# Gate logits and phi(K) column sums: from 128-column to 512-column matmuls in a gated mix of softmax and linear attention

## The chip, the cores and the metric

The kernel runs on one core of a Trainium2 chip. The core has five engines that each work through a queue of their own: TensorE (PE, matmuls, with its weight loads shown as PEld), VectorE (DVE), ScalarE (ACT), GpSimd (POOL) and SyncE (SP, which issues transfers). They work on SBUF, and matmuls write into eight PSUM banks of 128 partitions x 512 fp32 values. The metric is the device time of one launch in microseconds (us); lower is better. Six runs of the kernel before gave a median of 783.94 us, from 782.10 to 785.14.

## The reference

The input x has 2048 rows of 512 values. Two attention blocks read it, both with 32 heads of 16 values, and a gate mixes their results row by row:

```
g = sigmoid((x * gate_w).sum(-1))               # one number per row
a = softmax(q k^T / 4) v, heads joined, @ A_wo   # q, k, v = x @ A_wqkv
phi(t) = where(t > 0, t + 1, exp(t)) + 1e-6
kv = phi(k)^T v        (16 x 16 per head)        # q, k, v = x @ B_wqkv
z  = sum over rows of phi(k)
b = (phi(q) kv) / (phi(q) z + 1e-6), heads joined, @ B_wo
out = g * a + (1 - g) * b
```

The change touches two small things of this: the 2048 gate logits `x . gate_w`, and the 512 sums `z` of phi(K) over the rows.

## The kernel before

**Softmax attention.** There are 32 rounds: 4 chunks of 512 queries, in each 4 groups of 8 heads, in each group the even and the odd heads (4 heads at a time). In a round, 16 blocks of 128 keys x 4 heads give 64 score tiles of 128 x 512, one PSUM bank each. PE makes a score tile with a 32-row matmul; four of them can run at once in different rows of the array. Banks 0 to 4 belong to ACT: it takes tiles in groups of three and two and turns them into exponentials (line 908). PE multiplies those by V into bank 7, where a round accumulates.

**VectorE's share of the exponentials.** VectorE claims whole key blocks of a round, from block 15 downwards. It moves four score tiles out of the spare banks 5 and 6, one or two banks at a time (line 1151), and forms the exponential by integer steps (lines 1174, 1177, 1180, 1183: the "chain"). Each block it claims takes four tiles off ACT; PE then needs three products with V in place of one.

**Everything else** is a list of tasks that use banks 5 and 6 as well: projections K, Q and V (`t_kproj`, `t_qproj`, `t_v0`, `t_v1`), the gate (`t_gate`), phi(K) (`t_phik`), its sums (`t_z`), the 512 x 512 product G = x^T phi(K) (`t_g`), and the tail of the linear block and the output. At the end of a round VectorE transposes bank 7 (`round_end`, line 998), and every second round a task divides by the softmax sum and multiplies by the gate (`t_norm`), which waits for the gate task and reads the gate in the layout of 32x32 blocks (`gT`, 128 x 64). The linear block's denominator (`t_den`) reads the other gate factor with a row per partition (`g1`, 128 x 16).

**The order** is written out by a planner when the program is built. It keeps a clock for each engine, adds the `cost` of every instruction, and at each step gives PE the best candidate that is ready. Each engine then runs its list in order, waiting on semaphores. A task has a due time and a time before which it may not start, in rounds (the two numbers of `add(...)`); tasks are tried in the order of their due times. When a task that is due within `RES` rounds still needs a bank (`pressed`, line 1081), VectorE's claims leave one of the two spare banks free. Where PE is found to have spare time, matmuls on a constant tile `warm` are inserted.

**The gate before.** `gwb` holds gate_w copied 128 times. For each of the 16 row blocks, 4 matmuls of 128 columns take x as the stationary operand and `gwb` as the moving one, so that each row's logit lands on its own partition, in 128 equal columns; the next row block is written one column further, and column tb remains. ACT forms exp(-logit) from PSUM (line 533), VectorE the sigmoid and its complement (lines 536 to 538), and sixteen copies of 32 partitions x 16 bring it into the block layout `gT` (line 542).

**The sums before.** `t_z` does the same: 64 matmuls of 128 columns with phi(K) as the stationary operand and a tile of ones as the moving one, and one copy of 128 x 4 (line 591). GpSimd then scales masks with it into `Zsel`, which `t_den` uses.

Of the kernel before, what the change touches and what calls it, by code (L numbers as in the profile page):

```python
# [7 lines left out]
ACT = mybir.ActivationFunctionType  # L8
ALU = mybir.AluOpType
FP32 = mybir.dt.float32  # L10
# [135 lines left out]
def bass_gated_mix__mha_block__linear_attn_block__prompt_kernel(  # L146
# [14 lines left out]
    NTB = S // 128  # L161
    NQC = S // 512
    NCC = D // 128
# [9 lines left out]
    with ExitStack() as es:  # L173
        def SB(name, shape, dt):
            return es.enter_context(nc.sbuf_tensor("sb_" + name, list(shape), dt))
# [4 lines left out]
        xT = SB("xT", [128, NCC, S], BF16)  # L180
# [30 lines left out]
        mtmp = SB("mtmp", [128, 8], FP32)  # L211
        mask8 = SB("mask8", [128, 8], FP32)
        blockmask = SB("blockmask", [128, 128], BF16)
        eg = SB("eg", [128, NTB], FP32)
        g0 = SB("g0", [128, NTB], FP32)
        g1 = SB("g1", [128, NTB], FP32)
        gT = SB("gT", [128, NTB * 4], FP32)
        rden = SB("rden", [128, 2, 16], FP32)
# [22 lines left out]
        R = _Res  # L241
# [39 lines left out]
        r_gw = R("gw")  # L281
        r_gwb = R("gwb")
        r_eg = R("eg")
        r_g0 = R("g0")
        r_g1 = R("g1")
        r_gT = R("gT")
        r_rden = R("rden")
# [6 lines left out]
        def op(E, fn, reads=(), writes=(), cost=0.2):  # L294
            if E is DV:
                ev = E.add(fn, _deps_for(E, reads, writes), cost=max(cost - 0.084, 0.05), lag=min(0.084, cost - 0.05))
            else:
                ev = E.add(fn, _deps_for(E, reads, writes), cost=cost, lag=0.12 if E is AC else 0.0)
            _record(E, ev, reads, writes)
            return ev  # L300
# [43 lines left out]
        def pe(fns, reads=(), writes=(), waves=1.0, m="full", cols=None):  # L344
            deps = _deps_for(PE, reads, writes) + fdeps
            fdeps.clear()
            n = len(fns)
            first = None
            cost = mcost(m, waves)
            mode[0] = m  # L350
            for k, fn in enumerate(fns):
                ev = PE.add(fn, deps if k == 0 else (), inc=(k == n - 1), cost=cost / n, lag=0.155)
                if k == 0:
                    first = ev
            first.t = ev.t
            c = 512.0 * waves if cols is None else cols
            hist.append((PE.clock, c))
            COLS.append((PE.clock, c))
            hsum[0] += c
            for res in reads:  # L360
                res.r[PE] = first
            for res in writes:
                res.w = ev
                res.r = {}
            if filler[0]:
                filler[0] = False
                lastf[1] = ev
            return ev

        def mm(o, l, r, start=True, stop=True, sg=False):  # L370
            return lambda: nc.tensor.matmul(o, lhsT=l, rhs=r, start=start, stop=stop, skip_group_check=sg)  # L371
# [75 lines left out]
        def proj_steps(b, lhs, rhs, reads, w=512):  # L447
            for h2 in range(2):
                yield ("pe", reads, [r_bk[b]] if h2 == 0 else [], 2 * w / 512)
                pe([mm(BK[b][:, 0:w], lhs(cc), rhs(cc), start=(cc == 0), stop=(cc == NCC - 1)) for cc in (2 * h2, 2 * h2 + 1)],  # L450
                   reads=reads, writes=[r_bk[b]], waves=2 * w / 512)
# [14 lines left out]
        def t_kproj(t8, t):  # L466
            if t8 == 0:
                lhs, wr = (lambda cc: wA0[:, 0, cc, :]), r_wA0[0]
            else:
                lhs, wr = (lambda cc: wA[:, 1, cc, 128 * t8:128 * (t8 + 1)]), r_wA[1]  # L470
            b = yield "bank"
            yield from proj_steps(b, lhs, lambda cc: xT[:, cc, 512 * t:512 * (t + 1)], [r_xT[c][t] for c in range(NCC)] + [wr])
            yield ("dve", [r_bk[b]], [])
            op(DV, lambda: nc.vector.tensor_copy(KT[:, t8, 512 * t:512 * (t + 1)], BK[b]), reads=[r_bk[b]],
               writes=[r_KT[t8][t]], cost=0.69)
            yield "free"
# [41 lines left out]
        def t_v1(tb):  # L518
            b = yield "bank"
            yield from proj_steps(b, lambda cc: xT[:, cc, 128 * tb:128 * (tb + 1)], lambda cc: wA[:, 2, cc, 128:512],  # L520
                                  [r_xT[c][tb // 4] for c in range(NCC)] + [r_wv1], w=384)
            yield ("dve", [r_bk[b]], [])
            op(DV, lambda: nc.vector.tensor_copy(V[:, tb, 8:32, 0:Dh], BK[b][:, 0:384].rearrange("p (h d) -> p h d", d=Dh)),
               reads=[r_bk[b]], writes=[r_V[tb][1]], cost=0.56)
            yield "free"

        def t_gate():
            b = yield "bank"
            for tb in range(NTB):
                yield ("pe", xt_all + [r_gwb], [r_bk[b]] if tb == 0 else [], 1.0)  # L530
                pe([mm(BK[b][:, tb:tb + 128], xT[:, cc, 128 * tb:128 * (tb + 1)], gwb[:, cc, :], start=(cc == 0), stop=(cc == NCC - 1))
                    for cc in range(NCC)], reads=xt_all + [r_gwb], writes=[r_bk[b]], waves=1.1, cols=512)
            op(AC, lambda: nc.scalar.activation(eg[:], BK[b][:, 0:NTB], ACT.Exp, scale=-1.0), reads=[r_bk[b]], writes=[r_eg], cost=0.2)
            yield "free"
            yield ("dve", [r_eg], [])
            op(DV, lambda: nc.vector.tensor_single_scalar(g1[:], eg[:], 1.0, ALU.add), reads=[r_eg], writes=[r_g1], cost=0.08)
            op(DV, lambda: nc.vector.reciprocal(g0[:], g1[:]), reads=[r_g1], writes=[r_g0], cost=0.2)
            op(DV, lambda: nc.vector.tensor_tensor(g1[:], eg[:], g0[:], ALU.mult), reads=[r_g0, r_eg], writes=[r_g1], cost=0.1)
            gv = gT[:].rearrange("p (t a) -> p t a", a=4)
            for j in range(4):  # L540
                for a in range(4):
                    op(DV, lambda j=j, a=a: nc.vector.tensor_copy(gv[32 * j:32 * j + 32, :, a], g0[32 * a:32 * a + 32, :]),  # L542
                       reads=[r_g0], writes=[r_gT], cost=0.08)

        epos = [0]

# [35 lines left out]

        def t_z():
            b = yield "bank"
            for i in range(4):
                for h in range(4):
                    yield ("pe", r_phiK + [r_const], [r_bk[b]] if i == 0 and h == 0 else [], 1.0)
                    pe([mm(BK[b][:, i:i + 128], phiK[:, tb, 128 * i:128 * (i + 1)], ones[:], start=(tb == 0), stop=(tb == NTB - 1))
                        for tb in range(4 * h, 4 * h + 4)], reads=r_phiK + [r_const], writes=[r_bk[b]], waves=1.1, cols=512)
            yield ("dve", [r_bk[b]], [])  # L590
            op(DV, lambda: nc.vector.tensor_copy(zsb[:], BK[b][:, 0:4]), reads=[r_bk[b]], writes=[r_z], cost=0.17)
            yield "free"
            for i in range(4):
                op(PO, lambda i=i: nc.gpsimd.tensor_scalar(Zsel[:, 8 * i:8 * i + 8], mask8[:], zsb[:, i:i + 1], None, op0=ALU.mult),
                   reads=[r_z, r_mask], writes=[r_Zsel], cost=0.2)
# [108 lines left out]
        def add(key, gen, due, nb=-1.0, pre=()):  # L704
            t = Task()
            t.pre = list(pre)
            t.key, t.gen, t.due, t.nb, t.seq = key, gen, due, nb, len(bykey)
            t.bank, t.done, t.started = None, False, False
            t.req = next(gen)
            tasks.append(t)  # L710
            bykey[key] = t
            tasks.sort(key=lambda k: (k.due, k.seq))
# [310 lines left out]
        lastd = [False]  # L1023
        FILL = 1
        FILLC = 5200
        RES = .2
        CHG = .2
        CHI = 0.1
        CHI2 = 0.1
# [184 lines left out]
            round_check()  # L1214


        V1D = .7
        V1N = .3
        V1S = .05
        K1D = .6  # L1220
        MH2 = .9
        GD = 1.9
        GN = 1.5
        XT = [("xtr", t) for t in range(NQC)]
        for t in range(NQC):
            add(("xtr", t), t_xtr(t), 0.25 * t - 0.3)
# [2 lines left out]
                add(("Q", 0, 0), t_qproj(0, 0), -0.19, pre=[("xtr", 0)])  # L1229
            add(("V0", t), t_v0(t), 0.25 * t - 0.15, pre=[("xtr", t)])  # L1230
        for tb in range(NTB):
            add(("V1", tb), t_v1(tb), V1D + 0.05 * (15 - tb), V1N + V1S * (15 - tb), pre=XT)
        add(("gate",), t_gate(), GD, GN, pre=XT)
        for t8 in range(1, 4):
            for t in range(4):
                if t8 == 1:
                    due = K1D + (0, 0.5, 0.7, 0.1)[t]
                    add(("K", t8, t), t_kproj(t8, t), due, due - 0.3, pre=XT)
                    continue
                add(("K", t8, t), t_kproj(t8, t), 2 * t8 - 0.9 + 0.1 * t, 2 * t8 - 1.8 + 0.2 * t,  # L1240
                    pre=XT)
        for q4 in range(1, 16):
            qc, t8 = divmod(q4, 4)
            due = K1D + 0.05 if q4 == 1 else 2 * q4 - 0.9
            add(("Q", qc, t8), t_qproj(qc, t8), due, due - 0.6, pre=XT)
        for tb in range(NTB):
            add(("phiK", tb), t_phik(tb), 100 + tb, 2.5 + 0.65 * tb, pre=XT)
# [162 lines left out]
```

The softmax here doesn't subtract the row's maximum and nothing guards it: scores larger than these inputs give would overflow.

## Time and profile before

| | before |
|---|---|
| median of 6 runs | 783.94 us (782.10 to 785.14) |
| the profiled execution's own time | 784.43 us |
| its span, first to last instruction | 782.5 us |
| mean granted TensorE clock | 0.988 |
| ACT busy | 758.5 us, 97% |
| PE busy | 744.1 us, 95% |
| VectorE busy | 703.7 us, 90% |
| ACT exponentials of scores (line 908) | 653, 749.8 us |
| blocks claimed by VectorE (line 1180) | 104 |
| gate matmuls | 64, from 79.1 to 85.0 us |
| matmuls for z | 64, from 329.3 to 336.2 us |
| gate copies (line 542) | 16, 173 ns each |

The profile shows one execution. A group line gives the line of the program, engine, operation, output and inputs, the count, then busy us and mean ns of one, then the idle time of that engine just before these instructions and what ended most of it. A timeline line gives the start, the length, the engine, the line and a count of merged instructions, with the idle time before it in brackets. A window line gives start and end, then for each engine the busy us and the number of instructions, then the clock that TensorE was granted (1.00 is full), the share of DMA time and GB/s. All matmuls are recorded under line 371, since one helper issues them; they are told apart by their operands.

### The profile page before, as it was taken

What the parts mean: (1) busy time and instruction counts of PE and PEld (TensorE: products, weight loads), DVE (VectorE), ACT (ScalarE), POOL (GpSimd) and SP (SyncE); (2) the same over time, 40 slices, a digit from 0 to 9 for tenths busy, and PEclk for the clock granted to TensorE, in tenths of its full rate; (3) what the DMA queues carried; (4) which work ended last, traced back from release to release, by engine and by line L of the source; (5) the groups of instructions that cost most, each with busy time, mean ns of one, the idle gap of its engine ahead of it and who ended that gap; (6) DMA issues with size and microseconds to landing.
All of it is one profiled execution on the core that took longest, in us unless ns stands there. A gap on an engine that the chain in (4) does not pass through costs nothing.

```text
span 782.5 us, 18236 instructions
## 1 busy us (share of the span) xinstructions
PE 744.1 (95%) x7950; PEld 224.8 (29%) x7950; DVE 703.7 (90%) x997; ACT 758.5 (97%) x690; POOL 9.7 (1%) x36
## 2 busy tenths in 40 slices
PE   8999899999999999999999999999999999999997
PEld 3332322222222222332223223222322322232222
DVE  4498889899999999989999999989999998898995
ACT  5999899999999999999999999999999999999996
POOL 4000000000000000000000000000000000000000
PEclk9999999999999999999999999999999999999999
DMA  7200000000000000102002000100010011001000
GB/s 186 73 7 1 1 8 2 8 2 8 2 6 3 2 8 1 36 2 60 3 2 61 2 8 10 28 28 2 20 29 15 9 22 34 8 13 23 2 2 28
DMA packets 31343, 14.95 MB, mean 19 GB/s; under 512 B 19104, under 2 KB 31264, under 8 KB 31264
## 3 DMA queue, kind: packets, MB, share of 16 engines
q1 hardware_dynamic: 29392, 13.00, 6.4%
q8 instruction: 63, 1.03, 0.5%
q10 hardware_dynamic: 1872, 0.79, 0.4%
q14 instruction: 16, 0.13, 0.1%
HBM read 6.55 MB, written 2.10 MB: 11 GB/s over the span
## 4 chain that ended last, share of the span: by engine, by line
ACT 75%; PE 17%; DVE 4%; issue 2%; DVEq 0%; POOL 0%; ACTq 0%; POOLq 0%
ACT sb_PT L908 73%; PE ps L371 17%; ACT sb_ebuf L550 2%; DVE sb_Lb L1151 1%; DVE sb_Xb L1180 1%; DVE sb_gT L542 0%; DVE sb_Xb L1174 0%; DVE sb_Lb L1183 0%; DVE sb_Eb L1177 0%; DVE sb_OT L1017 0%; DVE sb_Tn L1013 0%; DVE sb_xnat L554 0%; DVE sb_U L998 0%; ACT sb_wA L676 0%; DVEq L1360 0%
## 5 line engine op out<-in xcount | busy, mean ns | idle before, releaser
L908 ACT ACTIVATE sb_PT<-ps 128x1536 bf16<-128x1536 f32 (+1 forms) x653 | 749.8, 1402 | 13.9 <-PE ps L371 13.4
L371 PE MATMUL ps<-sb_QP,sb_KT 32*128 32x512 bf16 x2048 | 308.3, 387 | 28.5 <-ACT sb_PT L908 14.8
L1151 DVE TENSOR_SCALAR sb_Lb<-ps 128x512 uint16<-128x512 f32 (+1 forms) x287 | 265.2, 925 | 39.1 <-PE ps L371 37.6
L371 PE MATMUL ps<-sb_warm 128*17 128x512 bf16 (+8 forms) x2142 | 203.1, 343 | 1.3 <-POOL sb_warm L409 1.3
L371 PEld LDWEIGHTS ps<-sb_QP,sb_KT 32*128 32x128 bf16 x2048 | 77.1, 91 | 284.8 <-ACT sb_PT L908 214.9
L371 PE MATMUL ps<-sb_PT,sb_V 128*17 128x512 bf16 x1632 | 156.4, 388 | 1.8 <-DVE sb_U L998 1.6
L1180 DVE TENSOR_TENSOR sb_Xb<-sb_Xb,sb_Lb 128x2048 bf16<-128x2048 bf16 x104 | 126.6, 1218 | 0.0
L371 PEld LDWEIGHTS ps<-sb_warm 128*17 128x17 bf16 (+2 forms) x2142 | 61.6, 91 | 48.2 <-issue 25.4
L1174 DVE TENSOR_SCALAR sb_Xb<-sb_Lb 128x2048 uint16<-128x2048 uint16 x104 | 71.5, 688 | 1.2
L1183 DVE TENSOR_SCALAR sb_Lb<-sb_Lb 128x2048 uint16<-128x2048 uint16 x104 | 71.3, 686 | 0.0
L1177 DVE TENSOR_SCALAR sb_Eb<-sb_Lb 128x2048 uint16<-128x2048 uint16 x104 | 71.3, 686 | 0.0
L371 PEld LDWEIGHTS ps<-sb_PT,sb_V 128*17 128x17 bf16 x1632 | 37.4, 87 | 100.6 <-issue 91.4
L371 PE MATMUL ps<-sb_Lb,sb_V 128*17 128x512 bf16 x416 | 40.8, 383 | 0.2
L371 PE MATMUL ps<-sb_Eb,sb_V 128*17 128x512 bf16 x416 | 40.8, 383 | 0.2
L371 PE MATMUL ps<-sb_Xb,sb_V 128*17 128x512 bf16 x416 | 40.8, 383 | 0.1
L371 PE MATMUL ps<-sb_xT,sb_wA 128*128 128x512 bf16 x108 | 32.1, 392 | 0.1
L998 DVE STREAM_TRANSPOSE sb_U<-ps 128x512 f32<-128x512 f32 x32 | 22.7, 709 | 7.7 <-PE ps L371 7.7
L550 ACT ACTIVATE sb_ebuf<-ps 128x512 bf16<-128x512 f32 x32 | 24.9, 777 | 0.0
L371 PE MATMUL ps<-sb_xT,sb_wBx 128*128 128x512 bf16 x64 | 18.8, 384 | 0.6 <-DVE sb_xnat L554 0.4
L371 PE MATMUL ps<-sb_wA,sb_xT 128*128 128x128 bf16 (+1 forms) x128 | 19.0, 275 | 0.2
L371 PE MATMUL ps<-sb_phiK 128*128 128x512 bf16 x64 | 19.0, 383 | 0.0
L371 PE MATMUL ps<-sb_wBx,sb_xT 128*128 128x512 bf16 x64 | 18.5, 384 | 0.0
(80 smaller groups left out, 301.7 us busy)
## 6 DMA issues: line engine op xcount, KB each, us to landing
sb_QP<-sb_QT SPq DMA_DIRECT2D x120, 16.0 KB, 1.8
out_dram<-sb_wA SPq DMA_DIRECT2D x14, 128.0 KB, 1.7
sb_wA<-in_A_wqkv_dram SPq DMA_DIRECT2D x2, 512.0 KB, 6.3
sb_wBx<-in_B_wqkv_dram SPq DMA_DIRECT2D x2, 512.0 KB, 6.0
sb_xnat<-in_A_x_dram SPq DMA_DIRECT2D x2, 512.0 KB, 3.9
sb_phiK<-sb_wA SPq DMA_TRANSPOSE x64, 2.4
sb_xnat<-in_A_x_dram SPq DMA_DIRECT2D x3, 256.0 KB, 3.0
sb_wBv<-in_B_wqkv_dram SPq DMA_DIRECT2D x1, 512.0 KB, 8.9
```

What stands on the lines that cost most here:

```text
L371: return lambda: nc.tensor.matmul(o, lhsT=l, rhs=r, start=start, stop=stop, skip_group_check=sg)
L550: op(AC, lambda: nc.scalar.activation(ebuf[:, s, :], BK[b], ACT.Exp), reads=[r_bk[b]], writes=[r_e[s]], cost=0.48)
L908: op(AC, lambda: nc.scalar.activation(PT[:, slot, 0:512 * n], ps[:, 512 * set_[0]:512 * (set_[0] + n)], ACT.Exp, scale=SCALE), reads=wr, w ...
L998: op(DV, lambda: nc.vector.transpose(U[:, par, :], acc), reads=[r_acc], writes=[r_U[par]], cost=0.71)
L1151: op(DV, lambda: nc.vector.tensor_scalar(Lb[:, sl, 512 * k:512 * (k + n)], src, S1A, S1B, op0=ALU.mult, op1=ALU.add), reads=[r_bk[b] for b ...
L1174: op(DV, lambda: nc.vector.tensor_scalar(X, L, 0x7F, 0x3F00, op0=ALU.bitwise_and, op1=ALU.bitwise_or), reads=[rl], writes=[rx], cost=CH[0])
L1177: ev = op(DV, lambda: nc.vector.tensor_scalar(E_, L, 0xFF80, None, op0=ALU.bitwise_and), reads=[rl], writes=[re_], cost=CH[1])
L1180: ev = op(DV, lambda: nc.vector.tensor_tensor(xb, xb, lb, ALU.mult), reads=[rx, rl], writes=[rx], cost=CH[2])
L1183: ev = op(DV, lambda: nc.vector.tensor_scalar(L, L, float(EXP_SH), None, op0=ALU.add), reads=[rl], writes=[rl], cost=CH[3])
```

## The change

The gate now keeps `gwb` as the stationary operand and streams x: for each of the four 512-row chunks, 4 matmuls of 512 columns put the 512 logits into a bank, the same on all 128 partitions. VectorE transposes the bank in 32x32 blocks into `rowt`, and a copy of every 32nd column brings 16 columns of the chunk into `gl`; since all partitions were equal, this is already the block layout. The exponential on ACT, and sum, reciprocal and product on VectorE, run on 128 x 64 values; the reciprocal writes `gT` directly, and four copies of 32 partitions x 16 make `g1`. The sums z go the same way: `ones` is stationary, 16 matmuls of 512 columns stream phi(K), one transpose and four copies make `zsb`.

Four planner numbers change with it: `RES`, and the due times and earliest starts of the second V projection, the second K projection, the second Q projection and the gate.

```diff
         def t_gate():
-            b = yield "bank"
-            for tb in range(NTB):
-                yield ("pe", xt_all + [r_gwb], [r_bk[b]] if tb == 0 else [], 1.0)
-                pe([mm(BK[b][:, tb:tb + 128], xT[:, cc, 128 * tb:128 * (tb + 1)], gwb[:, cc, :], start=(cc == 0), stop=(cc == NCC - 1))
-                    for cc in range(NCC)], reads=xt_all + [r_gwb], writes=[r_bk[b]], waves=1.1, cols=512)
-            op(AC, lambda: nc.scalar.activation(eg[:], BK[b][:, 0:NTB], ACT.Exp, scale=-1.0), reads=[r_bk[b]], writes=[r_eg], cost=0.2)
-            yield "free"
+            for t in range(NQC):
+                b = yield "bank"
+                rd = [r_xT[c][t] for c in range(NCC)] + [r_gwb]
+                yield from proj_steps(b, lambda cc: gwb[:, cc, :], lambda cc: xT[:, cc, 512 * t:512 * (t + 1)], rd)
+                yield ("dve", [r_bk[b]], [])
+                op(DV, lambda b=b: nc.vector.transpose(rowt[:], BK[b]), reads=[r_bk[b], r_gl], writes=[r_rowt], cost=0.71)
+                op(DV, lambda t=t: nc.vector.tensor_copy(gl[:, 16 * t:16 * (t + 1)], rowt[:].rearrange("p (b c) -> p b c", c=32)[:, :, 0]),
+                   reads=[r_rowt], writes=[r_gl], cost=0.17)
+                yield "free"
+            op(AC, lambda: nc.scalar.activation(eg[:], gl[:], ACT.Exp, scale=-1.0), reads=[r_gl], writes=[r_eg], cost=0.2)
             yield ("dve", [r_eg], [])
-            op(DV, lambda: nc.vector.tensor_single_scalar(g1[:], eg[:], 1.0, ALU.add), reads=[r_eg], writes=[r_g1], cost=0.08)
-            op(DV, lambda: nc.vector.reciprocal(g0[:], g1[:]), reads=[r_g1], writes=[r_g0], cost=0.2)
-            op(DV, lambda: nc.vector.tensor_tensor(g1[:], eg[:], g0[:], ALU.mult), reads=[r_g0, r_eg], writes=[r_g1], cost=0.1)
-            gv = gT[:].rearrange("p (t a) -> p t a", a=4)
-            for j in range(4):
-                for a in range(4):
-                    op(DV, lambda j=j, a=a: nc.vector.tensor_copy(gv[32 * j:32 * j + 32, :, a], g0[32 * a:32 * a + 32, :]),
-                       reads=[r_g0], writes=[r_gT], cost=0.08)
+            op(DV, lambda: nc.vector.tensor_single_scalar(gl[:], eg[:], 1.0, ALU.add), reads=[r_eg], writes=[r_gl], cost=0.17)
+            op(DV, lambda: nc.vector.reciprocal(gT[:], gl[:]), reads=[r_gl], writes=[r_gT], cost=0.6)
+            op(DV, lambda: nc.vector.tensor_tensor(gl[:], eg[:], gT[:], ALU.mult), reads=[r_gT, r_eg], writes=[r_gl], cost=0.2)
+            gv = gl[:].rearrange("p (t a) -> p t a", a=4)
+            for a in range(4):
+                op(DV, lambda a=a: nc.vector.tensor_copy(g1[32 * a:32 * a + 32, :], gv[32 * a:32 * a + 32, :, a]),
+                   reads=[r_gl], writes=[r_g1], cost=0.16)
...
         def t_z():
             b = yield "bank"
-            for i in range(4):
-                for h in range(4):
-                    yield ("pe", r_phiK + [r_const], [r_bk[b]] if i == 0 and h == 0 else [], 1.0)
-                    pe([mm(BK[b][:, i:i + 128], phiK[:, tb, 128 * i:128 * (i + 1)], ones[:], start=(tb == 0), stop=(tb == NTB - 1))
-                        for tb in range(4 * h, 4 * h + 4)], reads=r_phiK + [r_const], writes=[r_bk[b]], waves=1.1, cols=512)
+            for h in range(8):
+                rd = r_phiK[2 * h:2 * h + 2] + [r_const]
+                yield ("pe", rd, [r_bk[b]] if h == 0 else [], 2)
+                pe([mm(BK[b], ones[:], phiK[:, tb, :], start=(tb == 0), stop=(tb == NTB - 1)) for tb in (2 * h, 2 * h + 1)],
+                   reads=rd, writes=[r_bk[b]], waves=2)
             yield ("dve", [r_bk[b]], [])
-            op(DV, lambda: nc.vector.tensor_copy(zsb[:], BK[b][:, 0:4]), reads=[r_bk[b]], writes=[r_z], cost=0.17)
+            op(DV, lambda b=b: nc.vector.transpose(rowt[:], BK[b]), reads=[r_bk[b], r_gl], writes=[r_rowt], cost=0.71)
+            rv = rowt[:].rearrange("p (i j c) -> p i j c", i=4, j=4)
+            for j in range(4):
+                op(DV, lambda j=j: nc.vector.tensor_copy(zsb[32 * j:32 * j + 32, :], rv[32 * j:32 * j + 32, :, j, 0]),
+                   reads=[r_rowt], writes=[r_z], cost=0.16)
             yield "free"
...
-        RES = .2
+        RES = .5
...
-        V1D = .7
+        V1D = 1.3
         V1N = .3
-        V1S = .05
-        K1D = .6
+        V1S = .06
+        K1D = 1.3
         MH2 = .9
         GD = 1.9
-        GN = 1.5
+        GN = .5
...
-            add(("V1", tb), t_v1(tb), V1D + 0.05 * (15 - tb), V1N + V1S * (15 - tb), pre=XT)
+            add(("V1", tb), t_v1(tb), V1D + (0.05 * (15 - tb) if tb > 12 else V1S * (tb + 4)), V1N, pre=XT)
...
-                    due = K1D + (0, 0.5, 0.7, 0.1)[t]
-                    add(("K", t8, t), t_kproj(t8, t), due, due - 0.3, pre=XT)
+                    due = K1D + (0.3, 0.55, 0.8, 0)[t]
+                    add(("K", t8, t), t_kproj(t8, t), due, V1N, pre=XT)
...
-            due = K1D + 0.05 if q4 == 1 else 2 * q4 - 0.9
+            due = K1D + 0.25 if q4 == 1 else 2 * q4 - 0.9
```

More of the change, by code (lines that the diff above doesn't have):

```diff
@@ L213, in bass_gated_mix__mha_block__linear_attn_block__prompt_kernel @@
         blockmask = SB("blockmask", [128, 128], BF16)
-        eg = SB("eg", [128, NTB], FP32)
-        g0 = SB("g0", [128, NTB], FP32)
+        rowt = SB("rowt", [128, 512], FP32)
+        eg = SB("eg", [128, NTB * 4], FP32)
+        gl = SB("gl", [128, NTB * 4], FP32)
         g1 = SB("g1", [128, NTB], FP32)
@@ L283, in bass_gated_mix__mha_block__linear_attn_block__prompt_kernel @@
         r_eg = R("eg")
-        r_g0 = R("g0")
+        r_rowt = R("rowt")
+        r_gl = R("gl")
         r_g1 = R("g1")
```

## The prediction

> **What bounds the kernel now.** I read the page first: the busy shares, then the costliest groups.
>
> ```profile
> PE 744.1 (95%) x7950; PEld 224.8 (29%) x7950; DVE 703.7 (90%) x997; ACT 758.5 (97%) x690; POOL 9.7 (1%) x36
> ...
> L908 ACT ACTIVATE sb_PT<-ps 128x1536 bf16<-128x1536 f32 (+1 forms) x653 | 749.8, 1402 | 13.9 <-PE ps L371 13.4
> ```
>
> ScalarE (ACT) is the bound: 749.8 us of softmax exponentials, and only 13.9 us of idle in front of them. So a time can change in two ways: that idle, or the number of exponentials. The second is the trade that VectorE offers: each of the 104 key blocks that it claims (104 instructions of line 1180) takes four of the 2048 score tiles off ACT. The groups' other columns (shapes kept apart) count 326 exponentials of three tiles and 327 of two, 1632 tiles; the chain of waits shows 25 in a row (62 or 63 tiles) in 28.05 us from 537.07, 0.449 us a tile, so **a block is worth 1.80 us of ACT**. On VectorE it fills about 5.33 us, by the starts of successive instructions (0.60 for each of seven, 1.13 for the multiply).
>
> Next I asked where the 13.4 us of waiting lie: ACT's waits are ten, and 5.83 of them is the start. Windows of 5 us show the largest of the rest, behind the gate:
>
> ```profile
> core 0: us, PE busy (x) PEld busy (x) DVE busy (x) ACT busy (x) POOL busy (x), PEclk, DMA share, GB/s
> 80.00:85.00 5.00, 4.96 (x71) 3.49 (x67) 5.00 (x9) 5.00 (x6) 0.00 (x0) 1.00 0.02 3
> 85.00:90.00 5.00, 4.91 (x58) 1.27 (x55) 3.47 (x17) 5.00 (x7) 0.00 (x0) 1.00 0.00 0
> 90.00:95.00 5.00, 1.87 (x16) 0.52 (x18) 4.71 (x13) 2.97 (x3) 0.00 (x0) 0.94 0.00 0
> 95.00:100.00 5.00, 5.00 (x26) 0.84 (x26) 3.64 (x6) 2.80 (x3) 0.00 (x0) 0.50 0.00 0
> 100.00:105.00 5.00, 5.00 (x49) 1.29 (x47) 3.96 (x7) 4.77 (x5) 0.00 (x0) 0.88 0.04 11
> ```
>
> ACT is full to 90 us and loses 4.46 us in the next 15. TensorE (PE) is busy 1.87 of 5 us, and then runs at half clock. The timeline says why:
>
> ```profile
> 87.69 3.23 DVE L542 COPY sb_gT<-sb_g 32x16 f32<-32x16 f32 x16
> ...
> 90.95 0.69 DVE L1151 TENSOR_SCALAR sb_Lb<-ps 128x512 uint16<-128x512 f32 x1
> ...
> 91.79 0.40 PE L371 MATMUL ps<-sb_QP,sb_KT 32*128 32x512 bf16 x4 [1.88 <-DVE sb_Lb L1151]
> ...
> 92.23 2.37 ACT L908 ACTIVATE sb_PT<-ps 128x1536 bf16<-128x1536 f32 x2 [1.63 <-PE ps L371]
> ...
> 94.38 0.60 PE L371 MATMUL ps<-sb_PT,sb_V 128*17 128x512 bf16 x4 [1.33 <-DVE sb_U L998]
> ...
> 95.58 2.52 ACT L908 ACTIVATE sb_PT<-ps 128x1536 bf16<-128x1536 f32 x2 [0.98 <-PE ps L371]
> ...
> 99.67 2.53 ACT L908 ACTIVATE sb_PT<-ps 128x1536 bf16<-128x1536 f32 x2 [1.57 <-PE ps L371]
> ```
>
> Sixteen gate copies hold VectorE's queue for 3.23 us (0.20 apart, written into the program as 0.08 each). Behind them waits the line 1151 that frees a score bank; PE stands 1.88 us for it, and 1.33 us for the late transpose; the slow clock follows. ACT's waits here are 1.63, 0.98, 1.57 and 0.17: **4.35 us, all one event**. Three later ones (0.81, 0.78, 0.86 at 449, 568 and 711 us) are not near anything that changes.
>
> Here a page and the trace differ. The Trainium skill (TensorE: Matmul & The Clock Gate, "Why this matters for your kernels") wants no PE-idle gaps over about 3 us; here none exceeded 1.88 us and the clock still fell to 0.50. By the page's rule only the 1.63 would belong to the copies and the gain would be that much; I go by the trace's 4.35.
>
> **The change, part by part.**
>
> *PE.* Gate: 64 matmuls of 128 columns become 16 of 512. In a run, 16 of the first take 1.05 us (79.72 to the next group at 80.76), so 64 take 4.2; four 512-column ones from 31.11 last 1.03, of which the last takes 0.39, so 0.21 apart and 3.4 in all. 0.8 us less, and again 0.8 for z (64 to 16). ACT covers it: 5.00 of 5.00 busy while the gate's matmuls run, and no ACT wait between 326 and 345 us. Taken as 0; ends -1.6 and 0. The same skill page ("Wait — 56ns, not 53.3ns?") gives 55.6 and 215.7 ns, an estimate of only 0.1 us a task; nothing above needs it.
>
> *VectorE, gate.* Removed: 87.11 to 90.92, 3.81 us for 19 instructions. Added: four transposes of a bank, the form of line 998 (0.709), each with a copy behind it that waits for it (0.17 to 0.20, like the small gate instructions); with 0.03 of hand-over, 0.94 a pair, 3.76. Then the add (0.20), the reciprocal of 64 elements (0.253 for 16 and 0.953 for 128 give 0.55), the product (0.174 for 16, 0.293 for 128: 0.23) and three hand-overs, 1.08; four 32-partition copies at 0.20, 0.81. Sum 5.65, 1.84 more.
> *VectorE, z.* One copy (0.154) becomes a transpose and four copies, 0.74 + 0.81 = 1.55: 1.40 more. POOL's Zsel starts that much later; it ends at 338 us and the first denominator is finished at 479, so 140 us cover it.
> Each of the five transposes waits in VectorE's queue for its matmuls, and line 1151 pieces stand behind it; the casts of K (line 474) wait likewise, 1.0 us for nine after 30 us, so 0.11 apiece, 0.55 for five, which is 0.2 us of ACT and inside the ends below. The gate held one of the two spare banks from 79.1 to 85.8; it now holds one four times for some 2 us, which I count as equal.
> Together 3.2 us. VectorE is 90% busy, in the middle rounds 95%, so I make it pay in blocks: 3.2/5.33 x 1.80 = **+1.1 us** (ends: 0 if it fits its 79 us of idle; 3.6 for two whole blocks).
>
> *The stall.* The added pieces are larger but come as 4 x 0.94, separated by the matmuls of the next quarter, and a tail of 1.9; the costs written for them (0.71, 0.17, 0.6, 0.16) are near the rows, so the written order of PE no longer runs 2 us ahead of VectorE. **-4.35 us** (ends: -4.86, with the 0.51 wait at 78.21; -2.7, if PE's first wait of 1.63 stays and only the slow clock goes). What is late next is the exponential below.
>
> *A new wait.* Line 533 read PSUM straight behind PE and waited for nothing. Now ACT's gate exponential waits in ACT's queue for VectorE's last copy, and all softmax exponentials stand behind it. VectorE may be in a multiply (1.22) ahead of transpose and copy (0.88): 2.1, less the one exponential that ACT has in hand (1.19 or 1.61): **+0.6 us** (ends 0 and 2.1), once.
>
> *The order written for rounds 1 to 3.* V1 keeps 16 casts of 0.554 us and their matmuls, but key blocks 0, 1, 2 ... come due first, as the second head group eats them (three for VectorE's claims ahead), not last; K1's dues move too. Between 33 and 130 us VectorE finishes 10 blocks; at the later 20 per 130 us it would be 15; its 13.8 us of idle from 30 to 130 (86.2 busy by windows of 10 us) hold two blocks at most. I take half a block, **-0.9 us** (ends -3.6 and +1.8, a block lost). Every Q task's eight DMAs stay; they move with their dues.
>
> *RES .2 to .5.* A bank is kept from VectorE earlier before each due task. I take 0: a task that gets the bank starts at once. Its price is a rival below.
>
> Sum: -4.35 + 1.1 + 0.6 - 0.9 + 0 = -3.55 us. The profiled execution took 784.43 (span 782.5 and 1.93 around it), so 780.9 against it; it stood 0.49 above the median, 783.94, and against that **780.4**.
>
> **Rivals.**
> *A: the sum*, 780.4. Chance 0.45, its own range 777.5 to 782.8.
> *B: the order gains more.* The two blocks come that VectorE's early idle has room for, and not half: 2.7 more, 777.7; with the new wait fully hidden 777. For it: 40 single-bank pieces of line 1151 against 3 pairs between 30 and 130 us, 8.1 us idle before them. Against: PE is 5.00 of 5.00 there. Chance 0.20.
> *C: the stall moves.* Another late VectorE piece stops PE at another place, as at 449, 568 and 711 us without any gate; a fresh order may carry four more of about 0.85, 3.4, and 783.8 is left. Chance 0.14.
> *D: slower, the kept bank.* One round is 782.5/32 = 24.4 us, so RES keeps a bank up to 0.3 x 24.4 = 7.3 us longer for each of 27 K and Q tasks, if the task leaves it unused. In that time VectorE starts 1.1 blocks, 2.2 pairs of tiles that become singles: 2 x (0.686 + 0.17 idle) - (1.218 + 0.09) = 0.40 us each, 24 us in all, 4.5 blocks, 8.1 us: 788.5 at worst. It outweighs the sum's gain from 44% of that; at 75%, 786.5. For it: 129 pairs are there to be split, and PE's order has PE and ACT ahead of such tasks. Against: a free bank costs a task nothing to take. Chance 0.21.
> That PE's saving shortens nothing is part of all four.
>
> **How the numbers follow.** A measurement of this kernel tells about 0.2% (1.6 us) from no change. Faster: nearly all of A and all of B, 0.65. Same: C's middle and A's weak edge, 0.13. Slower: D and C's bad edge, 0.22. Range: down to 774.5 (B with VectorE's extra work and the wait both hidden, 1.7 less, and PE's 1.6), up to 787.5, most of D; the gains and losses share it, A's own range stands above.
>
> **What the profile after would show.** The sixteen copies gone; the ACT wait behind the gate under 1 us and the clock 1.00 through 85 to 105 us; four line-998-like transposes of 0.71 for the gate and one for z; a short ACT idle before the gate's exponential, released by VectorE; line 1180 at 103 to 105. Wrong: a count of 101 or less with more single-bank 1151s (D), new PE waits with half clock elsewhere (C), or 106 and more (B).

## The result and the profile after

The changed kernel takes 779.59 us (median of 19 runs), the kernel before 783.48 us in the same sessions (42 runs). The ratio, taken over all runs, is 0.9955, 95% interval [0.9945, 0.9964]: about 0.45% faster; that of the two medians is 0.9950. The forecast was 780.4 against 783.94, a ratio of 0.9955 as well. How much of that agreement was earned is the question of the rest. Of all executions below only two lie far outside, 1188 and 816 us, both of the last kernel of section 6: its time leaves them out, and as the profiled one is among them, its waits aren't known.

The page of the changed kernel, engine totals and the exponentials (busy us, share of the span; idle before them and what ended it):

```profile
PE 741.6 (95%) x7817; PEld 220.1 (28%) x7817; DVE 706.8 (91%) x999; ACT 757.8 (97%) x690; POOL 10.2 (1%) x36
...
L916 ACT ACTIVATE sb_PT<-ps 128x1536 bf16<-128x1536 f32 (+1 forms) x653 | 749.4, 1414 | 9.3 <-PE ps L373 9.1
...
L1188 DVE TENSOR_TENSOR sb_Xb<-sb_Xb,sb_Lb 128x2048 bf16<-128x2048 bf16 x104 | 126.6, 1218 | 0.0
```

There are still 653 exponentials and 104 claimed blocks. The span is 4.6 us shorter (777.9 after 782.5), and most of it is idle time: 9.3 us in front of the exponentials, where it was 13.9. VectorE has 3.1 us more to do. PE has 2.5 us less, but not by the shorter gate: the matmuls of gate and z are busy 9.4 us before and 9.3 after, and the filler on `warm` went from 203.1 to 194.1.

Behind the gate, windows of 5 us of the changed kernel (start:end, then for each engine busy us and instructions, then TensorE's clock, DMA share, GB/s):

```profile
75.00:80.00 5.00, 4.85 (x46) 1.61 (x38) 4.59 (x13) 4.00 (x6) 0.00 (x0) 1.00 0.00 0
80.00:85.00 5.00, 4.61 (x41) 1.09 (x39) 4.95 (x9) 4.68 (x5) 0.00 (x0) 1.00 0.00 0
85.00:90.00 5.00, 5.00 (x54) 1.69 (x53) 3.76 (x7) 4.65 (x5) 0.00 (x0) 1.00 0.01 3
90.00:95.00 5.00, 4.88 (x43) 1.27 (x39) 3.65 (x7) 5.00 (x5) 0.00 (x0) 1.00 0.00 0
95.00:100.00 5.00, 5.00 (x45) 1.37 (x42) 5.00 (x9) 5.00 (x6) 0.00 (x0) 1.00 0.07 17
```

PE is never below 4.61 of 5 us and its clock stays at 1.00. ACT still loses 1.67 us here, in four pieces (0.66, 0.34, 0.32, 0.35); its timeline names them (start, length, line, idle before and what ended it):

```profile
76.88 0.26 ACT L539 ACTIVATE sb_eg<-sb_gl 128x64 f32<-128x64 f32 x1 [0.66 <-DVE sb_gl L536]
...
78.82 3.28 ACT L916 ACTIVATE sb_PT<-ps 128x1024 bf16<-128x1024 f32 x3 [0.34 <-PE ps L373]
82.42 6.89 ACT L916 ACTIVATE sb_PT<-ps 128x1536 bf16<-128x1536 f32 x6 [0.32 <-PE ps L373]
89.65 21.79 ACT L916 ACTIVATE sb_PT<-ps 128x1536 bf16<-128x1536 f32 x19 [0.35 <-PE ps L373]
```

The 0.66 is the new wait of the gate's exponential for VectorE. The other waits after the start are 0.18 at 42 us (and 0.22 at 23.5, as before), 0.39 and 0.63 near 237 us, 0.89 at 470 us.

### The profile page after: what moved, and what is told of

It reads as the page before. It is cut to its first block, busy times and chain, and to the rows that moved or that the text cites. A ratio compares the mean times of both kernels' runs of the same rounds, so it can differ in the third digit from the quotient of the medians.

```text
span 777.9 us, 17928 instructions
## 1 busy us (share of the span) xinstructions
PE 741.6 (95%) x7817; PEld 220.1 (28%) x7817; DVE 706.8 (91%) x999; ACT 757.8 (97%) x690; POOL 10.2 (1%) x36
## 4 chain that ended last, share of the span: by engine, by line
ACT 81%; PE 11%; DVE 5%; issue 2%; DMA 1%; SPq 0%; DVEq 0%; ACTq 0%
ACT sb_PT L916 79%; PE ps L373 11%; ACT sb_ebuf L554 2%; DVE sb_Lb L1159 2%; DVE sb_Xb L1188 1%; DMA sb_xT<-in_A_x_dram 1%; DVE sb_Eb L1185 0%; DVE sb_Xb L1182 0%; DVE sb_Tn L1021 0%; DVE sb_xnat L558 0%; DVE sb_U L1006 0%; DVE sb_OT L1025 0%; SPq L306 0%; DVE sb_Lb L1191 0%; ACT sb_wA L684 0%
## 5 line engine op out<-in xcount | busy, mean ns | idle before, releaser
L373 PE MATMUL ps<-sb_warm 128*17 128x512 bf16 (+8 forms) x2105 | 194.1, 341 | 1.3 <-POOL sb_warm L411 1.3
L373 PEld LDWEIGHTS ps<-sb_warm 128*17 128x17 bf16 (+2 forms) x2105 | 59.8, 91 | 49.6 <-issue 27.7
```

## The experiments

Two readings compete from the start. The theory: the order that is written out for PE believed the sixteen gate copies took 0.05 us each of VectorE, they take 0.20, and what follows in PE's list came up to 2.4 us too early; the change removes this mis-booking. Rivals: the new planner numbers made the gain (rival 1), or the shorter work did, the matmuls of 512 columns and the missing copies (rival 2). All times below are medians; every group of runs had its own runs of the kernel before beside it, from 783.26 to 783.48.

### 1. One number in the kernel before

```diff
-                       reads=[r_g0], writes=[r_gT], cost=0.08)
+                       reads=[r_g0], writes=[r_gT], cost=0.284)
```

(VectorE's booked time is the cost less 0.084 and at least 0.05.)

> The kernel before, with one number changed: the sixteen gate copies are booked at 0.20 us of VectorE's time each, as measured, where a written cost of 0.08 books 0.05. The work is the same. Theory (it is the lateness against the written order that stalls PE, not the 3.2 us of copies): ACT's waits behind the gate fall below 1.5 us, the clock stays at 1.00, about 780.5. Rival 2 (what counted is that the copies, or the 128-column matmuls, are gone): within 1 us of before, 783.5.

Measured: **779.46 us, ratio 0.9954 [0.9937, 0.9970]**: the whole gain of the change, with not one instruction changed in kind. Windows, and VectorE's timeline, of this kernel:

```profile
85.00:90.00 5.00, 4.95 (x59) 1.33 (x56) 3.47 (x17) 5.00 (x7) 0.00 (x0) 1.00 0.00 0
90.00:95.00 5.00, 4.07 (x34) 1.13 (x31) 4.48 (x12) 5.00 (x6) 0.00 (x0) 1.00 0.00 0
95.00:100.00 5.00, 5.00 (x42) 1.34 (x41) 4.11 (x7) 5.00 (x6) 0.00 (x0) 1.00 0.10 26
```

```profile
87.64 3.25 DVE L542 COPY sb_gT<-sb_g 32x16 f32<-32x16 f32 x16
90.92 0.35 DVE L1010 RECIPROCAL sb_rden<-sb_U 128x32 f32<-128x32 f32 x1
```

The copies still hold VectorE for 3.25 us, but no line 1151 stands behind them that PE waits for: the next instruction is the normalization. ACT is full, the clock stays at 1.00. The expected time was 780.5. Of the waits around the gate only the 0.51 at 78 us is left. But the gain is not the gate's alone: the three late waits (2.45 us in all) are gone too, and a new one came, 2.66 us of ACT at 333 us, where PE's list now runs fourteen matmuls of G in one go (the G burst):

```profile
332.31 3.19 PE L371 MATMUL ps<-sb_phiK,sb_xnat 128*128 128x512 bf16 x14
...
336.52 5.97 ACT L908 ACTIVATE sb_PT<-ps 128x1536 bf16<-128x1536 f32 x5 [2.66 <-PE ps L371]
```

### 2. The operations alone, and the numbers alone

The first kernel has the new `t_gate` and `t_z` with RES .2 and the old dues; the second the old two with RES .5 and the new dues.

> The new gate and z, with the planner numbers of before (RES .2, the old dues). Theory (the stall behind the sixteen gate copies was the loss): ACT's waits behind the gate fall from 4.35 us to under 1.5 us and the time to about 780, 0.4% below before. Rival 1 (the planner numbers made the gain): about 783.5, no change, with the waits moved and not gone.

> The gate and z of before, with the new planner numbers. Theory: the sixteen copies still hold VectorE 3.2 us, ACT still waits 3 us or more behind them, the time stays within 1 us of before, 782.5 to 784.5. Rival 1 (the planner numbers made the gain): about 779.6, with less than 1.5 us of ACT wait behind the gate.

The numbers alone: 783.18, ratio 1.0003 [0.9991, 1.0015], with 3.19 + 0.84 + 0.71 us of ACT waits behind the gate. As the theory had it. This execution also started late: its first wait is 7.50 us and not 5.83. The operations alone: **787.18, ratio 1.0053 [1.0035, 1.0071], slower**, which neither reading expected. The gate's waits shrank only to 0.51, 0.37 and 2.00 us. No sixteen copies are there, yet PE idles again behind the gate and its clock falls; its longest idle time in this stretch is 0.98 us, for a late transpose of bank 7:

```profile
90.00:95.00 5.00, 2.95 (x20) 0.79 (x18) 4.37 (x13) 5.00 (x7) 0.00 (x0) 0.99 0.00 0
95.00:100.00 5.00, 5.00 (x32) 0.78 (x28) 2.58 (x5) 3.17 (x3) 0.00 (x0) 0.50 0.07 16
```

```profile
94.87 0.60 PE L373 MATMUL ps<-sb_PT,sb_V 128*17 128x512 bf16 x4 [0.98 <-DVE sb_U L1006]
...
100.59 10.88 ACT L916 ACTIVATE sb_PT<-ps 128x1536 bf16<-128x1536 f32 x9 [2.00 <-PE ps L373]
```

The G burst was there again (2.04 us), and a new event at 569 us:

```profile
569.19 0.93 PE L373 MATMUL ps<-sb_phiK 128*128 128x512 bf16 x2 [3.17 <-DMA sb_phiK<-sb_wA]
...
570.71 2.52 ACT L916 ACTIVATE sb_PT<-ps 128x1536 bf16<-128x1536 f32 x2 [3.61 <-PE ps L373]
```

PE waits for DMA transposes of the linear block's output. On SyncE's queue they are issued from 562.54 us on, sixteen in 24.70 us, right behind eight QP transfers of 4.94 us; PE starts at 569.19, 6.65 us after the first was issued, so it does not wait for all of them. Neither half of the change gains by itself.

### 3. The copies brought back into the changed kernel

```diff
+            for j in range(4):
+                for a in range(4):
+                    op(DV, lambda j=j, a=a: nc.vector.tensor_copy(scr[32 * j:32 * j + 32, 16 * a:16 * a + 16], gT[32 * a:32 * a + 32, 0:16]),
+                       reads=[r_gT], writes=[r_scr], cost=0.08)
```

(`scr` is a scratch tile. In the second kernel the cost is 0.284.)

> The changed kernel with sixteen extra VectorE copies of 32 partitions x 16 into a scratch tile after the gate, booked at 0.05 us each as in before; nothing reads them. Theory: PE's written order runs some 2.4 us ahead of VectorE again, ACT waits 3 to 5 us behind the gate, about 783. If only VectorE's work counted, 3.2 us of it are 0.6 of a block: at most 1.1 us, 780.7. Rival 2 (the matmuls): 779.6.

> The same sixteen extra copies in the changed kernel as in the run with the copies brought back, but booked at 0.20 us of VectorE's time each, as they take. Theory (the written order ahead of VectorE is what costs): 779.5 to 781, with under 2.2 us of ACT wait behind the gate. Rival (3.2 us more work on VectorE cost the time): 783 or more, as when they were booked at 0.05.

Under-booked: 784.82, ratio 1.0022 [1.0006, 1.0038], 5.2 us above the changed kernel. The event is back where the copies are (79.59, 3.13 us on VectorE), with PE waiting 2.75 us, until 84.58, for a cast of V that stands behind them:

```profile
79.59 3.13 DVE L552 COPY sb_scr<-sb_gT 32x16 f32<-32x16 f32 x16
...
86.34 1.02 ACT L922 ACTIVATE sb_PT<-ps 128x1024 bf16<-128x1024 f32 x1 [2.70 <-PE ps L375]
...
88.71 2.36 ACT L922 ACTIVATE sb_PT<-ps 128x1536 bf16<-128x1536 f32 x2 [1.34 <-PE ps L375]
...
92.14 1.45 ACT L922 ACTIVATE sb_PT<-ps 128x1536 bf16<-128x1536 f32 x1 [1.07 <-PE ps L375]
```

Truly booked: the 2.70, 1.34 and 1.07 are gone, and the waits from 70 to 110 us add up to 2.04 (0.66, 0.35, 1.03). But the time is 783.26, ratio 1.0000 [0.9987, 1.0014]: the theory's number for the waits held and its number for the time did not. The new order brought the G burst (2.04) and a wait of 5.83 instead of 4.00 us at the tail. The 3.2 us of work cost no block: 104 again.

### 4. Which part of the numbers

The changed kernel with RES .2; then with RES .5 and the old dues:

> The changed kernel with RES back at .2. Theory (a bank kept early spares PE the forced finish of a half-done task, as in the G burst of 3.2 us seen around 333 us in two runs with RES .2): an ACT wait of 2 us or more returns with a burst of one task's matmuls, 781.5 to 784. Rival D of the prediction (a bank kept early costs VectorE pairs of tiles): more two-bank pieces than 127 and a time of 779 or less.

> The changed kernel with RES at .5, but the dues and earliest starts of the V, K and Q projections and of the gate as before. Theory (their order is worth half a block or less): 779.5 to 781, 104 blocks. Rival (their order is what lets the new gate pay): 784 or more, with ACT waits of 4 us or more between 75 and 105 us.

RES .2: **786.27**, ratio 1.0039 [1.0026, 1.0052]. The G burst costs ACT 2.05 us and the wait for the DMA transposes 3.97 + 1.34, as in the operations alone:

```profile
336.34 92.76 ACT L916 ACTIVATE sb_PT<-ps 128x1536 bf16<-128x1536 f32 x82 [2.05 <-PE ps L373]
568.17 2.53 ACT L916 ACTIVATE sb_PT<-ps 128x1536 bf16<-128x1536 f32 x2 [3.97 <-PE ps L373]
572.04 6.02 ACT L916 ACTIVATE sb_PT<-ps 128x1536 bf16<-128x1536 f32 x5 [1.34 <-PE ps L373]
```

Two-bank pieces (line 1151 taking two banks at once) are 129 against 127, and the blocks 104 in both: rival D's mechanism is there in sign (two pairs) and worth nothing. Old dues: 783.41, ratio 1.0003 [0.9989, 1.0016], between the two expectations. Around the gate it has the waits of the operations alone, 0.51, 0.38 and 2.00, with a clock of 0.50 from 95 to 100 us, and 103 blocks, one fewer. In the profiled executions ACT waits as long as in the changed kernel, 9.8 us in all; the block is 1.8 of the 2.7 us between the two spans, and the rest isn't explained.

### 5. True booking with the other numbers

The kernel before, with the true cost and RES .5; with the true cost and all the new numbers; with RES .5 alone:

```diff
-                       reads=[r_g0], writes=[r_gT], cost=0.08)
+                       reads=[r_g0], writes=[r_gT], cost=0.284)
...
-        RES = .2
+        RES = .5
```

> The kernel before with two numbers changed: the gate copies booked at 0.20 us and RES .5. Theory: the gate's waits stay gone, and the ACT wait of 2.66 us behind the G burst at 333 us goes too: 776.5 to 778, better than the changed kernel. If RES does nothing: 779.5. If the new matmuls were needed after all: 783.

> The gate and z of before, the copies booked at 0.20 us, and all the planner numbers of the changed kernel: it differs from the changed kernel in the operations alone. Theory (the operations themselves are worth nothing, the booking is): under 1.5 us of ACT wait behind the gate and 777 to 780.5, no slower than the changed kernel's 779.6. Rival (the new matmuls and transposes pay): 782 or more.

> The kernel before with RES .5 alone; the copies stay booked at 0.05 us. Theory: 3 us or more of ACT wait stay behind the gate, 782.5 to 784.5. If RES and not the booking made the run with both numbers fast: 779 to 780.

The first: **778.49, ratio 0.9936 [0.9916, 0.9956]**, the lowest median of all, though its interval overlaps those of the true booking alone and of the changed kernel. Its profiled execution, the fastest of the six (776.3 us), has a single ACT wait between 24 us and the tail, the 0.51 at 78 us; the list of ACT's waits for PE is

```profile
ACT sb_PT L908 <- PE ps L371: 6.6, 3, 5.8
ACT sb_wA L676 <- PE ps L371: 4.0, 1, 4.0
```

of which 5.8 are the start and 4.0 the tail. So numbers alone, in the old kernel, do as much as the change; that RES adds to the booking isn't shown by the times. The second: 781.35, ratio 0.9970 [0.9957, 0.9984], slower than expected. The copies come 14 us earlier, a line 1151 and two casts are behind them again, and ACT waits 2.26 us although they are booked truly; the G burst of 2.66 is there too:

```profile
73.68 3.25 DVE L542 COPY sb_gT<-sb_g 32x16 f32<-32x16 f32 x16
...
76.96 0.69 DVE L1151 TENSOR_SCALAR sb_Lb<-ps 128x512 uint16<-128x512 f32 x1
...
79.19 0.39 PE L371 MATMUL ps<-sb_QP,sb_KT 32*128 32x512 bf16 x2 [0.66 <-DVE sb_V L523]
...
79.83 25.98 ACT L908 ACTIVATE sb_PT<-ps 128x1024 bf16<-128x1024 f32 x23 [2.26 <-PE ps L371]
```

Here the true booking made the stall smaller (3.19 us and more with the short one, section 2) and did not remove it. The third: 784.85, ratio 1.0012 [0.9998, 1.0026]: 3.27 us behind the gate and 2.11 in a G burst. RES alone gains nothing.

### 6. z, and a booking that is a little short

The changed kernel with the old z; and the first kernel of section 5 with a cost of 0.25 in place of 0.284:

> The changed kernel with the z of before (64 matmuls of 128 columns, one copy). Theory: z lies beside ACT's work either way; until 325 us the order is the changed kernel's, behind it the order is another: 778.5 to 781. If z's matmuls paid: 781.5 or more; if VectorE's 1.4 us for z cost blocks: 105 blocks and 778 or less.

> The kernel before with RES .5 and the copies booked at 0.166 us in place of 0.20: the work is the same and the booking 0.5 us short in all. It shows how much a rewritten order moves by itself. Theory (only a lateness of some us stalls): 776.5 to 780, no gate event. If the time of an order is mostly luck: waits of 2 us or more at another place and 781 to 784.

The old z: 779.98, ratio 0.9947 [0.9928, 0.9967], 104 blocks, the waits of the changed kernel to 240 us but for the start, 7.60 us and not 5.81. z's part of the change can't be told from nothing. The slightly short booking: 779.23, ratio 0.9942 [0.9921, 0.9963], within the theory's range; whether it has a gate event can't be seen.

With the old operations, then, the three kernels that book the copies at 0.05 us take 783.2 to 784.9 us, and the four that book them at 0.17 or 0.20 take 778.5 to 781.4, each with an order of its own.

### The ledger

| kernel | span | ACT waits for scores and gate | span less waits |
|---|---|---|---|
| before | 782.5 | 13.4 | 769.1 |
| changed | 777.9 | 9.1 + 0.7 | 768.1 |
| operations alone | 784.9 | 15.6 | 769.3 |
| numbers alone | 781.2 | 13.5 | 767.7 |
| true booking | 777.2 | 9.2 | 768.0 |
| copies back, short | 781.7 | 13.2 + 0.7 | 767.8 |
| copies back, true | 780.8 | 9.7 + 0.7 | 770.4 (tail 1.8 longer) |
| old z | 778.7 | 10.0 + 0.7 | 768.0 |
| RES .2 | 783.1 | 14.5 + 0.6 | 768.0 |
| old dues | 780.6 | 9.8 | 770.8 (one block fewer, 1.8) |
| true booking, RES .5 | 774.4 | 6.6 | 767.8 |
| true booking, new numbers | 778.6 | 11.2 | 767.4 |
| RES .5 alone | 782.3 | 13.8 | 768.5 |

The waits are the totals of ACT's own list of waits, in one execution of each kernel. With the two notes taken off, thirteen kernels lie between 767.4 and 769.3: ACT's busy time is nearly the same in all (757.2 to 758.5 us, 760.2 with one block fewer), so what moves the span by several us is its waits. Work that was added on PE or VectorE costs only what it adds to them or takes in blocks.

The start is part of these waits, and it differs between executions: 5.8 to 6.3 us in ten of them, 7.5 to 7.7 in the numbers alone, the old z and RES .5 alone. The changed kernel and the old z have the same order there, and the same eight matmuls of PE take 1.89 us in one and 3.57 in the other:

```profile
6.46 1.89 PE L373 MATMUL ps<-sb_xT,sb_OT 128*128 128x512 bf16 x8 [0.82 <-DMA sb_xT<-in_A_x_dram]
```

```profile
6.49 3.57 PE L373 MATMUL ps<-sb_xT,sb_OT 128*128 128x512 bf16 x8 [0.72 <-DMA sb_xT<-in_A_x_dram]
```

So two spans can differ by 1.8 us with no difference in the order up to there; why the eight matmuls differ stays open. Behind the start ACT waits 7.5 us in the kernel before, 4.0 in the changed kernel and with the old dues, 3.4 with the true booking, 0.7 with RES .5 as well, and 9.3 in the changed kernel with RES .2.

## Why the prediction was right or wrong

**The stall, -4.35: the size was right, the reason only in part.** ACT's waits around the gate, with the 0.51 that the prediction gave as an end, went from 4.86 to 1.01 us, or to 1.67 with the new one. That a short booking of the copies makes such a stall is shown from both sides: booking them truly removed it with the copies in place (section 1), and booking new ones short brought it back (section 3). But the prediction credited the operations with all of it. With the new operations and the old dues (sections 2 and 4) 0.4 and 2.00 us of waits and a half clock are still there, behind a late transpose; they went only with the new dues. The term is the work of both together.

**The new wait of the gate's exponential, +0.6: right,** 0.66 measured.

**VectorE's extra work, +1.1: wrong.** The durations held (transposes 0.706, copies 0.176, reciprocal 0.552, product 0.226 us; 3.1 us busy against 3.2), but the price did not. The step that failed is "so I make it pay in blocks": 104 blocks were claimed before and after, and also with 3.2 us more (section 3). What came is the low end that the prediction gave, 0. In these kernels only the old dues lost a block.

**The order of rounds 1 to 3, -0.9: wrong as a sum.** Ten blocks finished between 30 and 130 us before and after, not half a block more. But the dues were not idle: with the old ones the changed kernel is 3.8 us slower, of which one block, 1.8 us, is accounted for, and the waits behind the gate come back.

**RES, 0: wrong for this kernel, and the largest miss.** With RES .2 the changed kernel takes 786.27, 6.7 us more, mostly through two events at 334 and 567 us that the kernel before does not have. The prediction looked for RES's price in blocks and pairs; it lies in where other tasks fall. It is no fixed price either: the same step gave 1.0 us in the truly booked old kernel (779.46 to 778.49, intervals that overlap) and lost 1.5 in the kernel before (783.35 to 784.85, not clear of noise). The G burst is there in three kernels with RES .2 and in three with .5, so RES is not its cause by itself; what is, and why the output is placed ahead of its DMA transposes, was not tested.

**The rest.** The two wrong terms, +1.1 and -0.9, cancelled. The span fell by 4.6 us: 3.6 are ACT's waits, 0.7 are a shorter busy time of ACT for the same 690 instructions, which no run explains. The three late waits (2.45 us) were taken as unchanged; others came in their place (0.39, 0.63, 0.89, 1.91 in all). So rival C happened in small, and the agreement to 0.1% is in part luck. Rival D is refuted for this kernel, B did not happen. PE's saving at 0 stands: no run shows a gain from it.

**What the change itself is worth** depends on what surrounds it. Against the old operations truly booked, the new ones are 1.8 us faster with the new numbers (779.59 and 781.35), 4.9 us slower with RES .5 and the old dues (783.41 and 778.49), and 7.7 us slower with the old numbers (787.18 and 779.46). The sign turns with the numbers, so what differs is the order that is written, and no run shows a gain of the 512-column matmuls by themselves.

## What to carry to other kernels

Where an order is written out from booked costs, compare each booked cost with its row in the profile first: a booking that is short by 0.15 us sixteen times stopped TensorE for over 3 us and ScalarE for over 4, and correcting one number was worth as much as the change. True costs are no warrant, though: a stall of 2.26 us stood behind truly booked copies, and one of 2.00 in kernels without them. An engine's idle list tells more than its busy time here, since every edit rewrites the whole order. A forecast for such a kernel should hold several us for events at places that the edit does not touch, and one changed order is no measure of the operations in it.

## What the runs showed of the hardware

- A gap need not be long for the clock to fall. In the kernel before, PE idled 1.88 and 1.33 us within some 5 us and was granted 0.50 of its clock over the next window. With the operations alone no idle time of PE from 90 to 95 us was over 0.98 us, it was busy 2.95 of 5 us, and the next window had 0.50 too. A window with 3.74 of 5 us busy (75 to 80 us, true booking with the new numbers) was followed by 1.00.
- Sixteen VectorE copies of 32 partitions x 16 elements took 3.13 to 3.25 us in eight kernels, 0.20 us each from start to start, whether or not anything read them, though each was listed at 0.17.
- DMA transposes issued on SyncE's queue can be the end of a chain: in the run with the operations alone sixteen took 24.70 us to issue, behind 4.94 us of small transfers, and PE waited 3.17 us, until 6.65 us after the first was issued.
